# Moving the start addresses of the weight tiles and of x's low part in an attention and feed-forward kernel

## The chip, the cores and the metric

The kernel runs on one core of a Trainium2 chip. The time is device time of one execution in microseconds (us). The unchanged kernel took 599.97 us in the median of three runs (599.84 to 600.01).

The engines are named as the profile names them: PE is the matrix engine (a MATMUL streams columns, a LDWEIGHTS, shown as PEld, loads the stationary operand beforehand), DVE the vector engine, ACT the scalar engine, POOL the general engine, SP the engine that issues the transfers (DMA). Tiles lie in the core's own memory (SBUF, 128 partitions); sums of matmuls lie in PSUM. An address here is the byte within a partition at which a tile begins.

## The reference

Four batches of 768 tokens, eight heads of 64, go through chunked attention: each chunk of 32 queries sees 8 memory keys, 16 keys to its left, its own 32 and 8 to its right, 64 in all. The result, 3072 tokens of 512, is x of a feed-forward layer with 2048 hidden units:

```python
scores = scale * np.matmul(q_c, k_full.transpose(0, 1, 3, 2))
scores = scores - np.max(scores, axis=-1, keepdims=True)
a = np.exp(scores)
a = a / (np.sum(a, axis=-1, keepdims=True) + 1e-09)
out[:, :, c_start:c_end] = np.matmul(a, v_full)
...
h = x @ w_in
g = np.where(pos, h, np.where(neg, 0.0, (h + beta) ** 2 / (4.0 * beta)))
return (g @ w_out).astype(np.float32)
```

## The kernel before

The tokens are cut into six blocks of 512. A block's attention is done in two halves of 256 tokens: scores on PE, softmax on DVE and ACT, a transpose, values on PE, and then x of this half is written to SBUF as two tiles, a rounded high part `xth` (ACT, `x_high`) and the rest `xtl` (DVE, `x_low`). Each half is written by two instructions of DVE, `a` = 0 and 1, whose columns interleave in runs of 32; for the first block (`first_attention`) each of four pieces is written by one instruction, for two of the four groups of heads (`cc`) and one half. In a tile of x the four groups of 512 tokens follow each other.

The feed-forward layer runs over sixteen slices `fc` of 128 hidden units. A step `pe_hidden` is 12 matmuls of 512 columns: weights stand (high with x high, low with x high, high with x low, four groups `cc` each), x streams. After a gate on ACT and DVE, `pe_out` is 12 matmuls in which pieces of the gate's result `gh`, `gl` stand and 512 columns of weights stream. Every weight is held as a high and a low part too: sixteen tiles `w_0` to `w_15` arrive as raw words by DMA and are decoded in place by ACT and DVE (`decode`) into `wr` tiles under the same tags, 8192 bytes in a partition each: 4096 of high, 4096 of low, two of the 32 slices of weights in each (tile 0 holds the first two of `w_in`, the next ones a slice of `w_in` and one of `w_out`).

The order on every engine is written out: a string of names (`FIRST`) up to the end of the second block, a loop over steps after that. In the string, `g` is the first block's attention, `n` the others', `w` the decoding of a tile, `A` and `B` are steps of 256 tokens of the first block (its first and its second half), `J` steps of the whole of it, `C`, `D` and `E` the same of the second block. Nothing reorders it. What an instruction waits for is derived by the tile framework: an instruction that reads or writes a part of a tile waits for the earlier ones that touched parts which overlap it, by the views' offsets and strides as the framework sees them.

SBUF is filled pool after pool, tile after tile: `const` (the identity, then the weight tiles), `xpool` (two buffers each of `xth` and `xtl`), `apool` (attention's tiles), `gpool` (the gate's). The tile `offset` of 128 bytes at the head of `gpool` is never used. Line 63 of the profile is the helper that records all instructions, so groups are told apart by their tiles.

Of the kernel before, what the change touches and what calls it, by code (L numbers as in the profile page):

```python
# [9 lines left out]
F32R = mybir.dt.float32r  # L10
BF16 = mybir.dt.bfloat16
U32 = mybir.dt.uint32
# [4 lines left out]
P = 128  # L17
CHUNK, LEFT, RIGHT = 32, 16, 8
TB = 512
NCH = TB // CHUNK  # L20
NT = TB // P
NEG = -3.0e38
LAG = 2


STARTS = (3, 9)
# [42 lines left out]
def attn_ffn_kernel(ctx: ExitStack, tc: tile.TileContext, first_qk, first_v, qk, vw, w, out):  # L69
# [3 lines left out]
    NP = first_qk.shape[0]  # L73
# [9 lines left out]
    n2 = 2 * DM  # L83

    const = ctx.enter_context(tc.tile_pool(name="const", bufs=1))
    xpool = ctx.enter_context(tc.tile_pool(name="xpool", bufs=2))
# [44 lines left out]
    ws, raw = {}, {}  # L131

    def load_w(i, parts=(0, 1)):
        if i not in raw:
            raw[i] = const.tile([P, 2 * n2], U32, name=f"w_{i}", tag=f"w_{i}")
        a, b = parts[0] * n2, (parts[-1] + 1) * n2
        sp.dma_start(raw[i][:, a:b], w[i, :, a // 2 : b // 2].bitcast(U32))

# [5 lines left out]
    def words(i):  # L144
        pairs = raw[i].rearrange("p (n two) -> p n two", two=2)
        return pairs[:, :, 0], pairs[:, :, 1]

    def decode(i):

        low, u = words(i)  # L150
        high = u.bitcast(F32)

        act.activation(high, high, AF.Copy, scale=2.0**-112)
        yield
        f = apool.tile([P, n2], U32, name="f", bufs=2)
        dve.tensor_scalar(f, u, 3, None, op0=ALU.logical_shift_left)
        yield
        dve.scalar_tensor_tensor(f, low, 29, f, op0=ALU.logical_shift_right, op1=ALU.bitwise_or)
        yield
        dve.scalar_tensor_tensor(f, u, 0x80000000, f, op0=ALU.bitwise_and, op1=ALU.bitwise_or)  # L160
        yield
        f = f.bitcast(F32)
        ws[i] = const.tile([P, 2 * n2], F32R, name=f"wr_{i}", tag=f"w_{i}")
        hi, lo = ws[i][:, 0:n2], ws[i][:, n2 : 2 * n2]
        act.copy(hi, f)
        yield
        dve.tensor_tensor(lo, f, hi.bitcast(F32), op=ALU.subtract)
        yield


    scores_of, prob, prob_t, banks, xts, both = {}, {}, {}, {}, {}, {}

    def x_of(blk):
        if blk not in xts:
            xts[blk] = [xpool.tile([P, NP, TB], F32R, name=n) for n in ("xth", "xtl")]
        return xts[blk]

    def mask(c, s, swapped=False):
# [33 lines left out]
    def first_attention(g):  # L212
# [47 lines left out]
        for r in range(2):  # L260
# [14 lines left out]
        hi, lo = (  # L275
            x[:, 2 * u : 2 * u + 2, half * HT : (half + 1) * HT].rearrange("p r (t q) -> p r t q", t=2)
            for x in x_of(0)
        )
        act.copy(hi, src)
# [68 lines left out]
    def x_views(key, a):  # L348
        blk, half = key
        src = banks[key][:, a].rearrange("p (r t q) -> p r t q", r=NP, t=2)  # L350
        views = []
        for x in x_of(blk):
            x = x[:, :, half * HT : (half + 1) * HT].rearrange("p r (t a q) -> p r t a q", t=2, a=2)
            views.append(x[:, :, :, a])
        return (src, *views)
# [28 lines left out]
    def run(*chains):  # L384

        chains = [c for c in chains if c is not None]
        while chains:
            chains = [c for c in chains if next(c, chains) is not chains]
# [26 lines left out]
    def gating(s):  # L415

        h = hidden.pop(s)
        g = gpool.tile([P, TB], F32, name="gw", tag="gw")
        t = gpool.tile([P, TB], F32, name="gt")
        act.activation(g, h, AF.Relu, bias=0.5, scale=0.5)  # L420
        act.activation(t, h, AF.Relu, bias=-1.0)
        act.activation(g, g, AF.Square)
        gate[s] = (g, t)
# [12 lines left out]
    def gate_low(s):  # L436
        gh, gl = gs[s]
        dve.tensor_tensor(gl, gate.pop(s), gh.bitcast(F32), op=ALU.subtract)
        yield

    def pe_out(s):
        blk, fc = divmod(s, NFC)
        gh, gl = gs.pop(s)
        if fc == 0:
            pairs = [two_banks(f"a{i}", "ps_o") for i in range(NT // 2)]
            acc[blk] = [pairs[t // 2][:, t % 2] for t in range(NT)]
        wh, wl = weights(1, fc, 0), weights(1, fc, 1)
        pe_products(acc[blk], gh, gl, wh, wl, fc)
# [58 lines left out]
    def store(blk):  # L507
        for t in range(NT):
            src = acc[blk][t]
            if t % 2 == 0:  # L510
                ob = apool.tile([P, 2, DM], F32, name="ob", tag="f", bufs=2)
            dst = ob[:, t % 2]
            if t == NT - 1:
                dve.tensor_copy(dst[:, 0 : DM // 2], src[:, 0 : DM // 2])
                act.copy(dst[:, DM // 2 : DM], src[:, DM // 2 : DM])
            elif t % 2:
                act.copy(dst, src)
            else:
                dve.tensor_copy(dst, src)
            r0 = blk * TB + t * P  # L520
            sp.dma_start(out[r0 : r0 + P, :], dst)

    def keep_warm(n):
# [5 lines left out]

    early = [  # L530
        (load_first_qk, 0), (load_first_qk, 1), (load_first_v, 0), (load_w, 0), (load_first_v, 1),
        (load_first_qk, 2), (load_w, 1), (load_first_qk, 3), (load_first_v, 2), (load_first_v, 3),
        (load_w, 2), (load_w, 3), (load_w, 4), (load_qk, 1, 0), (load_v, 1, 0),
    ]
    early += [(load_w, i) for i in range(5, NPW)]
# [9 lines left out]
        "g": first_attention,  # L545
        "n": lambda i: attention((1 + i // 2, i % 2)),
        "w": decode,
    }
    parts = {"A": (0, (0, 1)), "B": (0, (2, 3)), "J": (0, range(NT))}
    parts |= {"C": (1, (0, 1)), "D": (1, (2, 3)), "E": (1, range(NT))}  # L550
    chains = {}
    for name in FIRST.split():
# [4 lines left out]
        if name not in chains:  # L557
            kind, i = name[0], int(name[1:])
# [15 lines left out]
    for s in range(first * NFC, steps):  # L574
# [25 lines left out]
        gating(s)  # L600
        if s - LAG >= first * NFC:
            pe_out(s - LAG)
            if (s - LAG) % NFC == NFC - 1:
                store((s - LAG) // NFC)
        else:
            n, i = LAST // LAG, s - first * NFC
            for name in items[len(items) - LAST :][i * n : (i + 1) * n]:
# [4 lines left out]
    run(gate_low(steps - 1))  # L612
    for s in range(steps - LAG, steps):
        pe_out(s)
# [90 lines left out]
```

## Time and profile before

| what | value |
|---|---|
| median of three runs | 599.97 us |
| the profiled execution | 600.11 us |
| its span, first to last instruction | 598.3 us |
| PE busy | 582.7 us, 97% |
| DVE busy | 325.6 us, 54% |
| ACT busy | 280.3 us, 47% |
| moved by DMA | 55.31 MB |

The page gives each engine's busy time; a view by stretches gives the same for any part of the span; the chain of waits follows the work that ended last back to the start, in pieces; the timeline lists instructions in order of time, equal neighbours merged ("x8"), with the start of the first. The time from one start to the next, over the count between them, is what a matmul costs in a stream: the duration of one is longer, because matmuls overlap.

### The profile page before, as it was taken

To read this page: it belongs to the slowest core of one execution; us is meant where nothing else is said; L and a number is where in the kernel's file an instruction comes from. 1 tells how busy PE (TensorE), PEld (TensorE's weight loads), DVE (VectorE), ACT (ScalarE), POOL (GpSimd) and SP (SyncE) were. 2 spreads that over 40 slices of the span, in tenths; PEclk is the share of its full clock that TensorE was granted. 3 is DMA by queue.
4 is the path that set the end of the run, shared out by engine and by line. 5 is a ranking of instruction groups with operands and counts; after the bars stand their busy time and mean duration, and the time that the engine had idled before them with its cause. 6 is when DMAs were issued, how large, how long until landed. Compare 5 with 4: busy or idle time off the path is not lost.

```text
span 598.3 us, 12265 instructions
## 1 busy us (share of the span) xinstructions
PE 582.7 (97%) x5496; PEld 483.5 (81%) x5496; DVE 325.6 (54%) x466; ACT 280.3 (47%) x503; POOL 0.7 (0%) x6
## 2 busy tenths in 40 slices
PE   5899999999999999999999999999999999999996
PEld 2888888788888888888888888888888888888885
DVE  5999999986474224636423644623564632322222
ACT  2689864554435335444435443434443444543442
POOL 0000000000000000000000000000000000000000
PEclk9999999999999999999999999999999999999999
DMA  8999300424051004012101223200310000100001
GB/s 355 422 418 419 148 1 0 178 82 168 1 177 71 0 1 158 26 65 108 71 1 71 107 71 107 71 1 34 144 71 2 1 2 0 71 0 1 0 1 70
DMA packets 9844, 55.31 MB, mean 92 GB/s; under 512 B 1088, under 2 KB 1088, under 8 KB 5184
## 3 DMA queue, kind: packets, MB, share of 16 engines
q1 hardware_dynamic: 9792, 54.53, 23.6%
q8 instruction: 43, 0.70, 0.5%
q14 instruction: 9, 0.07, 0.0%
HBM read 48.23 MB, written 6.29 MB: 91 GB/s over the span
## 4 chain that ended last, share of the span: by engine, by line
PE 82%; DVE 15%; issue 2%; DMA 1%; ACT 0%; DVEq 0%; ACTq 0%
PE ps_o L63 38%; PE ps_h L63 38%; DVE f L63 6%; PE ps_x L63 3%; DVE wr L63 2%; PE ps_s L63 2%; DVE gw L63 1%; DVE gl L63 1%; DVE pr L63 1%; DVE den L63 1%; DMA qk<-in_first_qk_dram 1%; DVE pt L63 1%; DVE mx L63 1%; DVE xtl L63 0%; DVE rin L63 0%
## 5 line engine op out<-in xcount | busy, mean ns | idle before, releaser
L63 PE MATMUL ps_h<-xth,wr 128*128 128x512 f32 (+1 forms) x832 | 195.6, 377 | 1.1 <-DVE wr L63 1.1
L63 PE MATMUL ps_o<-wr,gh 128*128 128x512 f32 x768 | 194.7, 390 | 0.0
L63 PEld LDWEIGHTS ps_h<-xth,wr 128*128 128x128 f32 x832 | 149.0, 190 | 30.3 <-DVE wr L63 1.5
L63 PEld LDWEIGHTS ps_o<-wr,gh 128*128 128x128 f32 x768 | 143.3, 188 | 29.4
L63 DVE SCALAR_TENSOR_TENSOR gw<-gw,gt 128x512 f32<-128x512 f32 (+1 forms) x104 | 67.2, 649 | 164.9 <-ACT gw L63 164.6
L63 ACT ACTIVATE gw<-ps_h 128x512 f32<-128x512 f32 (+1 forms) x104 | 58.6, 563 | 159.0 <-PE ps_h L63 158.9
L63 PE MATMUL ps_o<-wr,gl 128*128 128x512 f32 x384 | 106.9, 389 | 0.0
L63 PE MATMUL ps_h<-xtl,wr 128*128 128x512 f32 (+1 forms) x416 | 104.8, 374 | 0.0
L63 DVE TENSOR_TENSOR gl<-gw,gh 128x512 fp32r<-128x512 f32 (+1 forms) x104 | 67.4, 649 | 65.8 <-ACT gh L63 65.7
L63 ACT CAST gh<-gw 128x512 fp32r<-128x512 f32 (+1 forms) x104 | 61.1, 590 | 69.9 <-DVE gw L63 69.9
L63 PEld LDWEIGHTS ps_h<-xtl,wr 128*128 128x128 f32 x416 | 75.3, 190 | 13.9
L63 PEld LDWEIGHTS ps_o<-wr,gl 128*128 128x128 f32 x384 | 72.1, 188 | 15.1
L63 ACT ACTIVATE gw<-gw 128x512 f32<-128x512 f32 (+1 forms) x104 | 62.4, 600 | 0.0
L63 ACT ACTIVATE gt<-ps_h 128x512 f32<-128x512 f32 (+1 forms) x104 | 58.3, 561 | 0.0
L63 DVE STREAM_TRANSPOSE pt<-pr 32x512 f32<-32x512 f32 (+1 forms) x60 | 41.2, 698 | 1.3
L63 DVE SCALAR_TENSOR_TENSOR f<-w,f 128x1024 uint32<-128x1024 uint32 x32 | 39.0, 1220 | 0.4
L63 ACT ACTIVATE pr<-pr 128x1024 f32<-128x1024 f32 (+1 forms) x14 | 13.1, 937 | 35.1 <-DVE pr L63 35.0
L63 PEld LDWEIGHTS ps_x<-pt,v 64*64 64x64 f32 x1536 | 25.1, 142 | 5.0 <-issue 3.3
L63 PE MATMUL ps_x<-pt,v 64*64 64x32 f32 x1536 | 26.6, 226 | 1.2 <-ACT pt L63 1.2
L63 ACT CAST xth<-ps_x 128x512 fp32r<-128x512 f32 x24 | 13.1, 591 | 20.6 <-PE ps_x L63 20.6
L63 ACT CAST wr<-f 128x1024 fp32r<-128x1024 f32 x16 | 16.8, 1051 | 11.7 <-DVE f L63 11.7
L63 PEld LDWEIGHTS ps_s<-qk 64*32 64x32 f32 x1536 | 17.1, 112 | 6.1 <-issue 3.1
(27 smaller groups left out, 182.6 us busy)
## 6 DMA issues: line engine op xcount, KB each, us to landing
w<-in_w_dram SPq DMA_DIRECT2D x16, 1024.0 KB, 19.8
qk<-in_qk_dram SPq DMA_DIRECT2D x10, 1536.0 KB, 6.5
v<-in_vw_dram SPq DMA_DIRECT2D x10, 1024.0 KB, 5.5
out_dram<-ob SPq DMA_DIRECT2D x24, 256.0 KB, 2.0
qk<-in_first_qk_dram SPq DMA_DIRECT2D x4, 768.0 KB, 8.7
v<-in_first_v_dram SPq DMA_DIRECT2D x4, 512.0 KB, 12.7
```

Source lines behind the costliest of these rows:

```text
L63: return self.tc.keep_in_program_order(getattr(self.engine, name)(*args, **kwargs))
```

## The change

Every weight tile is made 16 bytes longer than is used, and so is the low part of x, whose used part begins 16 bytes into its tile. The allocator rounds a tile's size up to 32 bytes, so each weight tile begins 8224 bytes behind the one before it in place of 8192.

```diff
+STEP = 4
...
-            raw[i] = const.tile([P, 2 * n2], U32, name=f"w_{i}", tag=f"w_{i}")
+            raw[i] = const.tile([P, 2 * n2 + STEP], U32, name=f"w_{i}", tag=f"w_{i}")[:, 0 : 2 * n2]
...
-        ws[i] = const.tile([P, 2 * n2], F32R, name=f"wr_{i}", tag=f"w_{i}")
+        ws[i] = const.tile([P, 2 * n2 + STEP], F32R, name=f"wr_{i}", tag=f"w_{i}")[:, 0 : 2 * n2]
...
-            xts[blk] = [xpool.tile([P, NP, TB], F32R, name=n) for n in ("xth", "xtl")]
+            low = xpool.tile([P, NP * TB + STEP], F32R, name="xtl")[:, STEP:]
+            xts[blk] = [xpool.tile([P, NP, TB], F32R, name="xth"), low.rearrange("p (c t) -> p c t", c=NP)]
```

In the built programs the starts within 256 bytes are these:

| tiles | before | after |
|---|---|---|
| the sixteen weight tiles | 128, all | 128, 160, 192, 224, 0, 32, ... each 32 further, twice round |
| `xth`, two buffers | 128 | 192 |
| `xtl`, two buffers (used part) | 128 | 144 and 176 |
| `gh`, `gl` and the gate's others | 128 | 192 |

No instruction is added to the arithmetic or taken from it, and on every engine the instructions stand in the order they had. What changes beside the addresses is what some of them wait for. The first place is on DVE, in the second block's second half: the two instructions of `x_low`, and the gate's work around them.

```order
L63 TENSOR_TENSOR gl<-gw,gh 128x256 [waits DVE_49,Activation_49]
L63 SCALAR_TENSOR_TENSOR gw<-gw,gt 128x256 [waits Activation_49]
L63 TENSOR_TENSOR xtl<-ps_x,xth 128x4x2x64 [waits PE_49,Activation_49]
L63 TENSOR_TENSOR xtl<-ps_x,xth 128x4x2x64
L63 TENSOR_TENSOR gl<-gw,gh 128x256 [waits Activation_49]
```

and of the change:

```order
L64 TENSOR_TENSOR gl<-gw,gh 128x256 [waits DVE_49,Activation_49]
L64 SCALAR_TENSOR_TENSOR gw<-gw,gt 128x256 [waits Activation_49]
L64 TENSOR_TENSOR xtl<-ps_x,xth 128x4x2x64 [waits PE_49,Activation_49]
L64 TENSOR_TENSOR xtl<-ps_x,xth 128x4x2x64 [waits DVE_49]
L64 TENSOR_TENSOR gl<-gw,gh 128x256 [waits Activation_49]
```

The second write of x's low part now waits for a count of DVE's own, that of the first write; the same holds for all ten pairs of `x_low`.

The second place is on PE, at the same time in the program. `wr_398`, `wr_542`, `wr_593` and `wr_281` are the decoded tiles 1, 2, 3 and 0. The step with `xth,wr_542` is one of the second block's first half (`C`), the one with `xth,wr_281` behind it the first of its second half (`D`).

```order
L63 MATMUL ps_o<-wr_398,gl 128x512 [waits DVE_49]
L63 MATMUL ps_o<-wr_398,gl 128x512
L63 MATMUL ps_h<-xth,wr_542 128x256 x8
L63 MATMUL ps_h<-xtl,wr_542 128x256 x4
L63 MATMUL ps_o<-wr_542,gh 128x512 x4
L63 MATMUL ps_o<-wr_542,gl 128x512 x2
L63 MATMUL ps_h<-xth,wr_281 128x256 [waits Activation_49]
L63 MATMUL ps_h<-xth,wr_281 128x256 x7
L63 MATMUL ps_h<-xtl,wr_281 128x256 [waits DVE_49]
L63 MATMUL ps_h<-xtl,wr_281 128x256 x3
```

and of the change:

```order
L64 MATMUL ps_o<-wr_398,gl 128x512 [waits DVE_49]
L64 MATMUL ps_o<-wr_398,gl 128x512
L64 MATMUL ps_h<-xth,wr_542 128x256 x8
L64 MATMUL ps_h<-xtl,wr_542 128x256
L64 MATMUL ps_h<-xtl,wr_542 128x256 [waits DVE_49]
L64 MATMUL ps_h<-xtl,wr_542 128x256 x2
L64 MATMUL ps_o<-wr_542,gh 128x512 x4
L64 MATMUL ps_o<-wr_542,gl 128x512 x2
L64 MATMUL ps_h<-xth,wr_281 128x256 [waits Activation_49]
L64 MATMUL ps_h<-xth,wr_281 128x256 x7
L64 MATMUL ps_h<-xtl,wr_281 128x256 x4
```

The wait for the count that the second write of the first place reaches stood at the first step of half two, which reads what was written. It now stands seventeen matmuls earlier, at the second of the four x-low matmuls of a step of half one, whose columns that write doesn't touch; the three x-low matmuls from there on, six of `pe_out` and eight with x high stand behind it.

The third place is on DVE in the first block: the write of x's low part for its second half, groups 0 and 1.

```order
L63 TENSOR_TENSOR pr_275<-pr_275,rin 128x512 [waits DVE_49]
L63 SCALAR_TENSOR_TENSOR f<-w_335,f 128x1024
L63 TENSOR_TENSOR xtl<-ps_x,xth 128x2x256 [waits Activation_49]
L63 SCALAR_TENSOR_TENSOR gw<-gw,gt 128x256
L63 SCALAR_TENSOR_TENSOR f<-w_335,f 128x1024 [waits DVE_49]
```

and of the change:

```order
L64 TENSOR_TENSOR pr_275<-pr_275,rin 128x512 [waits DVE_49]
L64 SCALAR_TENSOR_TENSOR f<-w_335,f 128x1024
L64 TENSOR_TENSOR xtl<-ps_x,xth 128x2x256 [waits PE_49,Activation_49]
L64 SCALAR_TENSOR_TENSOR gw<-gw,gt 128x256
L64 SCALAR_TENSOR_TENSOR f<-w_335,f 128x1024 [waits DVE_49]
```

The write now also waits for a matmul on PE: the second x-low matmul of the hidden step that stands just ahead of it in the program, on the first half's columns.

## The prediction

> **What bounds the kernel now.** I read the busy times first, then the chain of waits where the bound changes hands, the busy times by stretches, and the timeline of the engine found.
>
> ```profile
> span 598.3 us, 12265 instructions
> PE 582.7 (97%) x5496; PEld 483.5 (81%) x5496; DVE 325.6 (54%) x466; ACT 280.3 (47%) x503; POOL 0.7 (0%) x6
> ```
>
> PE is busy nearly throughout, though not always as the bound:
>
> ```profile
> 105.87 1.23 DVE wr L63
> 107.10 0.04 issue
> 107.14 2.11 PE ps_h L63 x8
> ...
> 27.00:107.00 80.00, 77.85 (x739) 65.90 (x738) 79.27 (x103) 59.57 (x104) 0.00 (x0) 1.00 0.49 203
> 107.00:133.00 26.00, 25.86 (x373) 22.29 (x374) 23.95 (x35) 12.80 (x27) 0.00 (x0) 1.00 0.35 132
> 133.00:150.00 17.00, 17.00 (x224) 15.16 (x223) 11.91 (x21) 8.12 (x23) 0.00 (x0) 1.00 0.45 162
> 190.00:598.00 408.00, 403.71 (x3215) 333.40 (x3213) 166.94 (x241) 169.85 (x304) 0.00 (x0) 1.00 0.13 46
> ```
>
> The columns of the stretches are length, then busy time of PE, PEld, DVE, ACT and POOL, the granted clock, the DMA engines' share and GB/s. Up to 107.1 us the chain runs over DVE (79.27 of 80 us busy); from 107.14 it is PE, which works all 17.00 us of 133 to 150 and 25.86 of 26 before. So a delay of DVE counts before 107.1, a delay of PE counts after it, in full, because no pause follows that could take it up.
>
> What does a matmul cost in that stream?
>
> ```profile
> 398.09 1.98 PE L63 MATMUL ps_o<-wr,gh 128*128 128x512 f32 x8
> 399.90 1.07 PE L63 MATMUL ps_o<-wr,gl 128*128 128x512 f32 x4
> 400.81 1.98 PE L63 MATMUL ps_h<-xth,wr 128*128 128x512 f32 x8
> 402.62 1.07 PE L63 MATMUL ps_h<-xtl,wr 128*128 128x512 f32 x4
> 403.53 1.98 PE L63 MATMUL ps_o<-wr,gh 128*128 128x512 f32 x8
> ...
> 29.41 1.22 PE L63 MATMUL ps_h<-xth,wr 128*128 128x256 f32 x8
> 30.46 0.64 PE L63 MATMUL ps_h<-xtl,wr 128*128 128x256 f32 x4
> 30.95 0.49 PE L63 MATMUL ps_h<-ident,pr 128*128 128x128 f32 x3
> ```
>
> From 398.09 to 403.53 start 24 matmuls: 226.7 ns each, the same for those in which weights stand and x streams (2.72 us for 12) and those in which the gate's tiles stand and weights stream (2.72). With 256 columns the four from 30.46 to 30.95 take 0.12 us each (their unrounded starts give 120.0). So 256 columns cost 106.7 ns, and 13.3 ns of each matmul don't depend on its length. That rest is all that an address can take away: whatever it does, 213.3 ns stay.
>
> **The change part by part: addresses.** In the kernel before, all operands of these streams begin at the same byte within 256, so this trace holds no matmul with another distance between what stands and what streams. It does show whether PE's reads suffer from others' accesses to SBUF, which come at all distances:
>
> ```profile
> 170.88 1.98 PE L63 MATMUL ps_h<-xth,wr 128*128 128x512 f32 x8
> 172.69 1.07 PE L63 MATMUL ps_h<-xtl,wr 128*128 128x512 f32 x4
> 173.60 1.98 PE L63 MATMUL ps_o<-wr,gh 128*128 128x512 f32 x8
> 175.41 1.07 PE L63 MATMUL ps_o<-wr,gl 128*128 128x512 f32 x4
> 176.32 0.39 PE L63 MATMUL ps_h<-xth,wr 128*128 128x512 f32 x1
> ...
> 171.04:176.48 5.44, 5.44 (x26) 4.50 (x25) 4.74 (x8) 2.96 (x5) 0.00 (x0) 1.00 0.45 183
> 398.25:417.29 19.04, 19.04 (x86) 15.77 (x85) 4.85 (x7) 8.86 (x16) 0.00 (x0) 1.00 0.00 1
> ```
>
> At 171 to 176 us DVE works 4.74 of 5.44 us and DMA moves 183 GB/s, at 398 to 417 DVE 4.85 of 19.04 and DMA 1 GB/s; 24 matmuls take 5.44 us (170.88 to 176.32) there and 5.44 here (398.09 to 403.53). Traffic that must meet PE's reads in the same memory at changing addresses costs nothing to the nanosecond. I therefore take 13.3 ns for a cost of changing the standing weights, not of addresses, and the change of addresses for 0. The bounds: 13.3 ns gained on every moved matmul, or the slowest run of eight lost:
>
> ```profile
> 113.31 2.12 PE L63 MATMUL ps_h<-xth,wr 128*128 128x512 f32 x8
> 115.27 1.08 PE L63 MATMUL ps_h<-xtl,wr 128*128 128x512 f32 x4
> 116.19 1.98 PE L63 MATMUL ps_o<-wr,gh 128*128 128x512 f32 x8
> ```
>
> behind the switch from scores, where eight take 1.96 us (245 ns, 18.3 over the rule, the refilling of PE among it) and the next four 0.92 (230 ns, 3.3 over): neighbours in kind of what another phase between loads and streams can cost. The matmuls at stake start after 107.14:
>
> ```profile
> L63 PE MATMUL ps_o<-wr,gh 128*128 128x512 f32 x672 | 170.1, 390 | 0.0
> L63 PE MATMUL ps_h<-xth,wr 128*128 128x512 f32 x620 | 155.3, 392 | 1.1 <-DVE wr L63 1.1
> L63 PE MATMUL ps_o<-wr,gl 128*128 128x512 f32 x336 | 93.4, 389 | 0.0
> L63 PE MATMUL ps_h<-xtl,wr 128*128 128x512 f32 x312 | 83.5, 389 | 0.0
> ```
>
> That is 1940; the weights' starts run twice round the eight places within 256, so two tiles of sixteen still agree with x high and the gate's tiles: 14/16, about 1700, change their distance. The bounds are -22.6 us (13.3 ns) and +31 us (18.3 ns), with 0 the value taken.
>
> [...]
>
> DVE, ACT and the DMAs meet other addresses too:
>
> ```profile
> L63 DVE SCALAR_TENSOR_TENSOR f<-w,f 128x1024 uint32<-128x1024 uint32 x32 | 39.0, 1220 | 0.4
> L63 DVE TENSOR_TENSOR pr<-pr,rin 128x1024 f32<-128x1024 f32 x10 | 12.3, 1225 | 0.3
> ACT w L63 <- DMA w<-in_w_dram: 1.2, 2, 1.1
> ```
>
> `f` begins at 0 within 256 and `pr` at 128; 1024 columns with two operands cost DVE 1220 and 1225 ns, so I take 0 for the engines (a bound is those 5 ns in 1225, some 0.3 us of the 79.27 that DVE works while it is the bound). The weight DMAs write as many bytes as before, and all that waits for them waits 1.2 us, in two waits. The upper bound is that these double, 1.2 us; the value is 0, because the loads' lengths stay.
>
> **The waits.** The new tile has 2052 words for 4 groups of 512 and begins 4 words in; the framework no longer sees that parts of it don't overlap. Three waits come of it.
>
> First, PE's at the step of the second block's first half:
>
> ```profile
> 133.23 0.64 PE L63 MATMUL ps_h<-xtl,wr 128*128 128x256 f32 x4
> 133.06 1.29 DVE L63 TENSOR_TENSOR xtl<-ps_x,xth 128x512 fp32r<-128x512 f32 x2 [0.54 <-ACT xth L63]
> ...
> 28.87 0.20 DVE L63 RECIPROCAL rin<-den 128x8 f32<-128x8 f32 x1
> 29.11 0.69 DVE L63 TENSOR_TENSOR pr<-pr,rin 128x512 f32<-128x512 f32 x1
> ```
>
> The second x-low matmul started at 133.23 + 0.12 = 133.35. It will wait for the second of the two writes, which here overlap (1.29 us for both). With the new wait between them the second starts when the first is done and its count is seen: 0.04 us, as from 28.87 + 0.20 = 29.07 to 29.11, where the one needs the other's result. So 133.06 + 0.69 + 0.04 + 0.68 = 134.47, and PE goes on 0.04 later (the "issue" between DVE wr and PE ps_h at 107.10): 134.51. That is 1.16 us of stall. After a pause PE refills: the eight from 29.41 to 30.46 take 1.05 where 8 x 0.12 = 0.96, so 0.09 more. **+1.25 us.** Behind it stand x-low matmuls, six of pe_out and the steps after them, all in the stream without a pause: nothing takes it up. Were the writes 1.16 us earlier, it would cost nothing; that is the lower bound. The upper one is 1.25 + 0.12, if ACT's writes of x high ahead come a little later too.
>
> Second, DVE's at the first block's second half:
>
> ```profile
> 29.72 1.22 DVE L63 SCALAR_TENSOR_TENSOR f<-w,f 128x1024 uint32<-128x1024 uint32 x1
> 30.85 0.68 DVE L63 TENSOR_TENSOR xtl<-ps_x,xth 128x512 fp32r<-128x512 f32 x1
> ```
>
> The write began 0.09 us before the f ahead of it had ended (30.94). It will wait for the second x-low matmul of 30.46, which starts at 30.58 and is over some 0.28 later (0.64 less 3 x 0.12), at 30.86, before the f. What goes is the overlap: **+0.1 us**, on DVE while it is the bound. Bounds 0 and 0.15.
>
> Third, the nine other pairs of x_low lose an overlap of some 0.12 us each on DVE after 107.1, when DVE pauses for hundreds of us in all and PE doesn't wait for it: 0. Were the cover gone, 9 x 0.12 = 1.1 us.
>
> Sum: 1.25 + 0.10 = 1.35 us on the profiled execution's 600.11 gives 601.5; it lies 0.14 over the median, so on 599.97 **601.3 us**, 0.22% more.
>
> **The rivals.** *Collisions at equal starts, now avoided.* For it: 13.3 ns are unexplained, and all operands did begin alike. Against it: other traffic at all distances costs PE nothing. Price: 1700 x 13.3 ns = -22.6 us, so 578.7; a mild form, 3.3 ns, gives -5.6 and 595.7.
>
> *Equal starts were the good case.* Loads and streams that ran in step now don't, and the stream settles at the 230 ns of 115.27 to 116.19: 1700 x 3.3 = +5.6 us, 606.9; it decides from 0.7 ns per matmul on, which outweighs the waits. For it: the rhythm does vary behind switches. Against it: it finds back to 226.7 within a dozen matmuls.
>
> *The waits cost next to nothing*, because the two writes of x low come earlier than I read them or PE makes up for it: 600.0 to 601.1, no change.
>
> **How the numbers follow.** About 0.2%, 1.2 us, is what a measurement of this kernel tells from none: slower begins at 601.2. Forecast (addresses nothing, waits 1.35) 0.45; waits less than that 0.17; equal starts were good 0.20; collisions avoided 0.18. The forecast's own range is 601.2 to 601.6. The range reaches to the mild form of both address rivals, 3.3 ns either way: 595.7 to 606.9, which leaves out about 0.08 above and 0.12 below. Faster 0.18, the same 0.17, slower 0.45 + 0.20 = 0.65.
>
> **What would show it.** Twelve matmuls at 2.72 us in all steps, with tiles of every start: addresses cost nothing; 2.56 would be the first rival, 2.76 and more the second, and steps that differ tile by tile would tell the distances apart. A pause of PE of about 1.2 us near 133 us that ends on DVE xtl, and pairs of xtl that no longer overlap, show the waits. I am wrong if the steps change their length, if no such pause is there, or if the bound changes hands later than 107.3.

## The result, and the profile after

The changed kernel takes 610.89 us in the median (610.59 to 611.11) beside 599.95 us for the kernel before on the same chip: a ratio of 1.0182, interval 1.0165 to 1.0200. It is slower by 10.9 us. The profiled execution took 610.81 us.

First the span and the busy times, of the changed kernel:

```profile
span 609.0 us, 12266 instructions
PE 592.5 (97%) x5496; PEld 483.0 (79%) x5496; DVE 326.6 (54%) x466; ACT 281.1 (46%) x503; POOL 0.7 (0%) x6
```

PE does the same 5496 matmuls and is busy 9.8 us longer (582.7 before); DVE and ACT have grown by 1.0 and 0.8 us. The span has grown by 10.7. Nearly all of it is work of PE that became longer, and little of it waiting. The stretches of the changed kernel show where:

```profile
107.00:133.00 26.00, 26.00 (x373) 22.07 (x372) 24.16 (x35) 13.14 (x28) 0.00 (x0) 1.00 0.36 132
133.00:150.00 17.00, 16.05 (x220) 14.18 (x219) 10.52 (x19) 8.14 (x23) 0.00 (x0) 1.00 0.49 174
190.00:609.00 419.00, 414.39 (x3224) 335.37 (x3222) 168.44 (x242) 171.32 (x307) 0.00 (x0) 1.00 0.12 45
```

Between 107 and 133 PE still did 373 instructions, as before. Between 133 and 150 it is idle for 0.95 us, where it had no pause. And the long rest of the program, from 190 us to the end, has grown from 408 to 419 us with nearly the same PE work in it (3224 instructions, 3215 before), at a granted clock of 1.00 as before. The chain of waits in the long rest, of the changed kernel (start, us, what):

```profile
396.33 2.79 PE ps_h L64 x12
399.13 2.80 PE ps_o L64 x12
401.92 2.81 PE ps_h L64 x12
404.73 2.79 PE ps_o L64 x12
407.52 2.78 PE ps_h L64 x12
410.30 2.80 PE ps_o L64 x12
413.11 2.77 PE ps_h L64 x12
415.88 2.74 PE ps_o L64 x12
```

Behind 190 us every step of twelve matmuls that doesn't follow a switch from the attention's small ones took 2.72 us before, whatever its tile (2.95 to 2.97 behind a switch). In this stretch it takes 2.74 to 2.81 now, and it differs from step to step: 0.06 us more in a typical step, 5 ns per matmul. I took the starts of the single matmuls out of both traces, paired them in the order of the program, and averaged the interval from one start to the next over all matmuls of 512 columns behind 107.1 us that are followed by another such one, without the first interval behind a pause or a switch (18 before, 17 after, some 340 ns each; 1898 and 1900 intervals stay): **227.1 ns before, 232.0 ns after**. For the 1940 matmuls of that kind that is 1940 x 4.9 ns = 9.5 us. The delay of each matmul against its counterpart grows evenly, by about 0.5 us per hundred matmuls of 512 columns, apart from one jump.

The jump is the wait that the prediction named. Timeline of PE and of DVE, the row of the waits, and the chain of waits there, all of the changed kernel:

```profile
133.56 0.28 PE L64 MATMUL ps_h<-xtl,wr 128*128 128x256 f32 x1
134.78 0.62 PE L64 MATMUL ps_h<-xtl,wr 128*128 128x256 f32 x3 [0.95 <-DVE xtl L64]
...
133.31 1.42 DVE L64 TENSOR_TENSOR xtl<-ps_x,xth 128x512 fp32r<-128x512 f32 x2 [0.54 <-ACT xth L64]
...
PEld ps_h L64 <- DVE xtl L64: 1.2, 1, 1.2
...
133.31 0.70 DVE xtl L64
...
134.04 0.70 DVE xtl L64
...
134.78 0.62 PE ps_h L64 x3
```

One x-low matmul starts at 133.56, the next at 134.78, 1.22 us later in place of 0.12; the two writes of x low no longer overlap (1.42 us for the pair in place of 1.29). The delay of PE against the kernel before is 0.33 us just ahead of this pause, 1.55 at 135 us and 10.67 at the end. So 1.2 us are the pause with the refilling behind it, and 9.1 us come after it, which are the 1866 matmuls of 512 columns that stand there, at 4.9 ns each. The other 74 stand ahead of the pause; its end is set by DVE, so what they lose costs nothing. The chain runs over DVE, with a stretch of ACT at 131 us, until the second write ends at 134.74 us, where in the kernel before PE carried it from 107.14 on. On DVE 0.14 us of delay are there from the program's first 10 us on (the traces of other kernels lie between 0.4 us earlier and 0.14 later at that place), and 0.11 us come from the earlier pair of writes of x low, at 108.9 us.

### The profile page after: what moved, and what is told of

The parts are those of the page before. It is cut to its first block, busy times and chain, and to the rows that moved or that the text cites. A ratio compares the mean times of both kernels' runs of the same rounds, so it can differ in the third digit from the quotient of the medians.

```text
span 609.0 us, 12266 instructions
## 1 busy us (share of the span) xinstructions
PE 592.5 (97%) x5496; PEld 483.0 (79%) x5496; DVE 326.6 (54%) x466; ACT 281.1 (46%) x503; POOL 0.7 (0%) x6
## 4 chain that ended last, share of the span: by engine, by line
PE 79%; DVE 17%; issue 2%; DMA 1%; ACT 1%; DVEq 0%; ACTq 0%
PE ps_h L64 37%; PE ps_o L64 36%; DVE f L64 6%; PE ps_x L64 3%; DVE wr L64 2%; PE ps_s L64 2%; DVE gw L64 2%; DVE gl L64 2%; DVE pt L64 1%; DVE pr L64 1%; DVE den L64 1%; DVE mx L64 1%; DMA qk<-in_first_qk_dram 1%; DVE xtl L64 1%; DVE ob L64 0%
## 5 line engine op out<-in xcount | busy, mean ns | idle before, releaser
L64 PE MATMUL ps_o<-wr,gh 128*128 128x512 f32 x768 | 198.4, 395 | 0.0
L64 PE MATMUL ps_h<-xth,wr 128*128 128x512 f32 (+1 forms) x832 | 198.1, 380 | 0.0
L64 PE MATMUL ps_o<-wr,gl 128*128 128x512 f32 x384 | 108.9, 394 | 0.0
L64 PE MATMUL ps_h<-xtl,wr 128*128 128x512 f32 (+1 forms) x416 | 106.8, 378 | 0.9 <-DVE xtl L64 0.9
```

Of the source, the lines that this page charges most:

```text
L64: return self.tc.keep_in_program_order(getattr(self.engine, name)(*args, **kwargs))
```

## The experiments

Three theories stood at the start. *Distance*: what a matmul costs depends on how far apart, within 256 bytes, its standing and its streaming operand begin. *Spacing*: it is the weight tiles' distance from one another, 8224 in place of 8192 bytes, or that steps of different starts follow each other. *Waits*: it is the new waits. A distance is given here as the start of the standing operand less that of the streaming one, within 256. It is 0 for all of these matmuls in the kernel before; in the changed kernel it goes through the multiples of 32 in the steps with x high and in `pe_out`, and through those 16 away from them with x low. The weight tiles lie in memory in the order in which the program first asks for them, which is 0, 13, 1, 14, 15 and then 2 to 12, and not by number.

### Longer spacing, equal starts

The change with 256 in place of 16 bytes: the tiles lie further apart, and all begin alike again.

```diff
-STEP = 4
+STEP = 64
```

> The same change with steps of 256 bytes in place of 16: every weight tile begins 8448 bytes behind the last, x's low part 256 bytes further, so all starts agree within 256 as before; the framework sees no overlap with this size, so the added waits are gone too. Theory D (a matmul costs more when the operand that streams and the operand that is loaded begin at different bytes within 256, by some 5 to 6 ns on average): 600.0 us, twelve matmuls at 2.72 us. Rival S (the spacing of the tiles itself, or that they are parts of longer tiles, costs): about 610 us.

Measured: 599.98 us beside 599.99, ratio 1.0000 (0.9991 to 1.0009). Its chain of waits:

```profile
398.00 2.72 PE ps_o L64 x12
400.72 2.72 PE ps_h L64 x12
```

The steps are back at 2.72 us. Longer tiles and another spacing, 8448 bytes or 33 times 256 from tile to tile, cost nothing that shows; for the loss, the starts within 256 bytes had to differ. The framework sees no overlap with this length either, and the pause near 133 us is gone as well.

### The weights alone

The weights as in the change, x low as before; no wait is added.

```diff
-            low = xpool.tile([P, NP * TB + STEP], F32R, name="xtl")[:, STEP:]
-            xts[blk] = [xpool.tile([P, NP, TB], F32R, name="xth"), low.rearrange("p (c t) -> p c t", c=NP)]
+            xts[blk] = [xpool.tile([P, NP, TB], F32R, name=n) for n in ("xth", "xtl")]
```

> Weight tiles 32 bytes further on from one to the next, x low as before, no added wait. Theory D: 14 of 16 tiles differ from x and from the gate's tiles, 1940 matmuls at a mean of 231.8 ns in place of 226.7: 600.0 + 9.9, about 609.5 us, and no pause of PE near 133 us. Rival X (the shift of x low is what unsettles the stream): 600 us.

Measured: 610.08 us beside 599.99, ratio 1.0166 (1.0149 to 1.0183). Its chain of waits:

```profile
412.25 2.75 PE ps_h L64 x12
415.00 2.79 PE ps_o L64 x12
417.79 2.73 PE ps_h L64 x12
```

The weights' starts alone bring 10.1 us, and the steps differ tile by tile as in the changed kernel: the mean interval is 232.3 ns, and 1940 x 5.2 ns = 10.2 us. With x low moved as well it is 232.0, a little less: moving x low cost nothing further once the weights were moved, beyond its waits.

### The low part of x alone

Only x low begins further on, at 144 and 176; x high, the weights and the gate's tiles stay at 128 (the unused tile ahead of the gate's was cut by 64 bytes for that). The waits are those of the change.

```diff
-            xts[blk] = [xpool.tile([P, NP, TB], F32R, name=n) for n in ("xth", "xtl")]
+            high = xpool.tile([P, NP, TB], F32R, name="xth")
+            low = xpool.tile([P, NP * TB + 4], F32R, name="xtl")[:, 4 : 4 + NP * TB]
+            xts[blk] = [high, low.rearrange("p (c t) -> p c t", c=NP)]
...
-    gpool.tile([P, 32], F32, name="offset", bufs=1)
+    gpool.tile([P, 16], F32, name="offset", bufs=1)
```

> x low alone begins 16 and 48 bytes further within 256 (two buffers), weights, x high and the gate's tiles all at 128 as before; the added waits are there. Theory D: the 312 matmuls of 512 columns that stream x low cost about 6 ns more, 1.9 us, and the waits 1.25: 603.1 us. Rival W (x low's address costs nothing, only its waits): 601.2 us. Rival X (x low unsettles the whole stream): 608 us or more.

Measured: 605.45 us beside 599.99, ratio 1.0090 (1.0075 to 1.0105), more than expected. Timeline of PE:

```profile
406.27 1.10 PE L63 MATMUL ps_h<-xtl,wr 128*128 128x512 f32 x4
407.21 2.00 PE L63 MATMUL ps_o<-wr,gh 128*128 128x512 f32 x8
409.05 1.07 PE L63 MATMUL ps_o<-wr,gl 128*128 128x512 f32 x4
409.95 1.98 PE L63 MATMUL ps_h<-xth,wr 128*128 128x512 f32 x8
411.77 1.09 PE L63 MATMUL ps_h<-xtl,wr 128*128 128x512 f32 x4
412.69 2.00 PE L63 MATMUL ps_o<-wr,gh 128*128 128x512 f32 x8
```

The four x-low matmuls, at a distance of 240 or 208 (x low has two buffers), take 0.94 us (406.27 to 407.21) or 0.92 (411.77 to 412.69) in place of 0.91. But the eight behind them, whose own distance is 0, take 1.84 us (407.21 to 409.05) in place of 1.81 as well; only the four `gl` after that are back at 0.90. One by one the eight take 230, 224, 231, 236, 228, 232, 231 and 227 ns: PE needs about eight matmuls to fall back into its old rhythm. About 0.026 us in each of 78 pairs of steps makes 2.0 us, and 312 x 5.7 ns = 1.8 us for the x-low matmuls themselves (232.4 ns in the mean); with 1.5 us of waits (next experiment) that is 5.3, measured 5.5. The direction was that of the distances; what a disturbed matmul does to its followers was missing from the expectation.

### The waits alone

x low is lengthened so that the framework sees the overlap, and padding puts every start back to 128.

```diff
-            xts[blk] = [xpool.tile([P, NP, TB], F32R, name=n) for n in ("xth", "xtl")]
+            high = xpool.tile([P, NP, TB], F32R, name="xth")
+            low = xpool.tile([P, NP * TB + 4], F32R, name="xtl", tag=f"xtl{blk % 2}", bufs=1)[:, 0 : NP * TB]
+            if blk < 2:
+                xpool.tile([P, 56], F32, name=f"pad{blk}", bufs=1)
+            xts[blk] = [high, low.rearrange("p (c t) -> p c t", c=NP)]
```

> The added waits without any other address: x low in tiles four words longer, filled up so that every start within 256 is as before. The prediction's term: one pause of PE of 1.2 us near 133 us, 601.2 us in all, twelve matmuls at 2.72 us. Rival: PE makes up for the pause later, 600.0 us; or the waits disturb the stream beyond the pause, over 602 us.

Measured: 601.51 us beside 599.99, ratio 1.0025 (1.0016 to 1.0034): 1.5 us. Timeline of PE, then its chain of waits:

```profile
132.99 0.28 PE L63 MATMUL ps_h<-xtl,wr 128*128 128x256 f32 x1
134.39 0.62 PE L63 MATMUL ps_h<-xtl,wr 128*128 128x256 f32 x3 [1.12 <-DVE xtl L63]
```

```profile
396.67 2.72 PE ps_h L63 x12
399.39 2.72 PE ps_o L63 x12
```

The pause is there, 1.40 us from start to start in this kernel (0.12 without the wait), and the steps stay at 2.72. So the waits are one part and the addresses another, and the waits are by far the smaller one.

### One distance for all: 128, and 192

If the distance counts, and not the change of distance from step to step, then a constant distance must cost as much. With 128 bytes ahead of x in its pool, x and the gate's tiles begin at 0 and the weights at 128: all these matmuls have a distance of 128.

```diff
+    xpool.tile([P, 32], F32, name="shift", bufs=1)
```

> One distance for all, other than 0: x and the gate's tiles begin 128 bytes further within 256 than every weight tile; no tile is longer, no wait added, nothing changes from one step to the next. Theory D (each distance has its own steady rhythm, and only 0 gives 226.7 ns): the settled intervals of the staggered kernels at distance 128, alternately 229 and 238 ns, mean 233.3, on all 1940 matmuls: 600.0 + 12.9 = about 613 us, twelve matmuls at 2.80 us. Rival U (the stagger unsettles the stream because the distance changes every twelve matmuls; one that stays is as cheap as 0): 600.0 us, 2.72 us.

And with 64 bytes ahead of x and a longer unused tile ahead of the gate's, x begins at 192, the gate's tiles at 64 and the weights at 128: a distance of 192 for all.

```diff
+    xpool.tile([P, 16], F32, name="shift", bufs=1)
...
-    gpool.tile([P, 32], F32, name="offset", bufs=1)
+    gpool.tile([P, 64], F32, name="offset", bufs=1)
```

> Weights begin 192 bytes further within 256 than x, the gate's tiles 192 further than the weights: one distance of 192 from what streams to what is loaded, everywhere. Theory D: the settled intervals at this distance in the staggered kernels, 226, 229 and 232 ns, mean 229.0: 600.0 + 4.5 = about 604.5 us. Rival U: 600.0 us. If distances had nothing to do with it but only how many bytes apart (64 is as far as 192 going round): as at distance 64, 233.3 ns, 612.9 us.

Measured: at 128, 610.20 us beside 599.93, ratio 1.0170 (1.0155 to 1.0186); at 192, 605.43 us beside 599.93, ratio 1.0095 (1.0080 to 1.0110). The chains of waits, of the kernel at 128 and of the one at 192:

```profile
401.11 2.78 PE ps_h L63 x12
403.89 2.78 PE ps_o L63 x12
```

```profile
398.29 2.77 PE ps_h L63 x12
401.06 2.75 PE ps_o L63 x12
```

In both kernels all weight tiles are 8192 bytes apart, no wait is added and every step has the same starts; still each step takes longer, by an amount that belongs to its distance. That rules out spacing, and the change from step to step, as what is needed. The size at 128 was expected too high, at about 613 us: the mean interval is 232.2 ns, not 233 and more, and 1940 x 5.1 ns = 9.9 us, measured 10.3. At 192 it is 229.9 ns: 5.4 us, measured 5.5.

### All starts moved together

64 bytes ahead of everything: all tiles begin at 192, and all distances stay 0.

```diff
+    const.tile([P, 16], F32, name="shift")
```

> Weights, x and the gate's tiles all begin 64 bytes further within 256, at 192: every distance is 0 as before, only the common start is another. Theory D (distance alone): 600.0 us, twelve matmuls at 2.72 us. Rival (the start itself counts, 128 being a good one): 604 us or more.

Measured: 600.14 us beside 600.10, ratio 1.0004 (0.9995 to 1.0013). Its chain of waits:

```profile
398.23 2.72 PE ps_o L63 x12
400.95 2.72 PE ps_h L63 x12
```

A common shift of 64 bytes costs nothing that shows: of the starts, it is the distance between them that counts in the shifts tried.

### Distances of a few bytes

The decoded weights begin 0, 4, 8 ... 60 bytes further on in their tiles, x and the gate's tiles stay. The distance is 0 to 56 in `pe_hidden`, where weights stand, and 252 to 196 in `pe_out`, where they stream (tile 0 holds weights of `pe_hidden` alone, tile 15 of `pe_out` alone). Here tiles are meant by number.

```diff
-        ws[i] = const.tile([P, 2 * n2], F32R, name=f"wr_{i}", tag=f"w_{i}")
+        ws[i] = const.tile([P, 2 * n2 + 64], F32R, name=f"wr_{i}", tag=f"w_{i}")[:, i : i + 2 * n2]
```

> The decoded weight tiles begin 0, 4, 8 ... 60 bytes further within 256, from tile 0 to tile 15; x and the gate's tiles stay; no wait added. It shows the distances below 64 in steps of 4 for steps of hidden, above 192 for pe_out. If lines of 16 bytes matter: tiles 0 to 3 at 2.72 us for twelve, the others at 2.75 to 2.80, about 608 us in all. If every byte matters: tile 0 alone at 2.72, about 610 us. If the start within 32 or 64 bytes is what counts and these are small: 600 to 603 us. A piece of twelve below 2.72 us would show a distance that is cheaper than 0.

Measured: 609.22 us beside 599.93, ratio 1.0154 (1.0137 to 1.0171); the mean interval of 231.9 ns times 1940 gives 9.3 us, as measured. Its chain of waits:

```profile
221.17 2.72 PE ps_o L63 x12
223.89 2.75 PE ps_h L63 x12
226.64 2.72 PE ps_o L63 x12
229.36 2.79 PE ps_h L63 x12
232.15 2.84 PE ps_o L63 x12
```

A distance of four bytes, 232.7 ns in the table below, is enough to lose the rhythm. From these kernels (the change, the weights alone, the three with a uniform or a fine distance) I read the interval of a matmul of 512 columns at each distance, as the mean over its runs of one kind once the rhythm has settled, in ns:

| distance, bytes | interval |
|---|---|
| 0 | 226.7 |
| 32, 64, 96 | 233.3, 233.3, 234.7 |
| 128 | 232.8 |
| 160, 192, 224 | 233.5, 228.9, 233.4 |
| 4, 8, 12, 16 | 232.7, 230.4, 230.0, 233.3 |
| 20, 24, 28, 36 | 233.3, 230.0, 233.3, 231.7 |
| 40, 44, 48 to 56 | 233.3, 230.0, 233.3 |
| 196, 200, 204, 208 | 226.7, 230.3, 233.3, 233.3 |
| 212, 216, 220, 228 | 230.0, 233.1, 234.8, 226.7 |
| 232, 236, 240, 244 | 233.3, 235.8, 230.2, 228.9 |
| 248, 252 | 233.8, 236.9 |

All lie between 226.7 and 237. Two further distances, 196 and 228, do as well as 0, and none does better. The means often stand for a period: at 128 the intervals alternate between 229 and 238, or repeat after eight or more. The multiples of 32 occur in both kinds of step and at 32, 64, 96, 160 and 224 agree between them within 1 ns. The other distances come from `pe_hidden` up to 56 and from `pe_out` from 196 on, but for the runs of four with x low.

Nor does the distance alone fix the interval. At 36 (`pe_hidden` with tile 9) the stream ran at 233 ns in three of the last four blocks and at 226.8 in the last, and the 231.7 of the table is a mean of the two. The chain of waits of this kernel, that step in the third block and in the last:

```profile
279.42 2.80 PE ps_h L63 x12
563.96 2.72 PE ps_h L63 x12
```

So one distance can have more than one rhythm. What decides which of them the stream takes, no run here tells.

### A second good distance

Is 228 as good as 0 for a whole kind of step? The gate's tiles begin 228 bytes further on, so all of `pe_out` has a distance of 228 and `pe_hidden` keeps 0.

```diff
-        gh = gpool.tile([P, TB], F32R, name="gh", bufs=3)
-        gl = gpool.tile([P, TB], F32R, name="gl", bufs=3)
+        gh = gpool.tile([P, TB + 64], F32R, name="gh", bufs=3)[:, 57 : 57 + TB]
+        gl = gpool.tile([P, TB + 64], F32R, name="gl", bufs=3)[:, 57 : 57 + TB]
```

> The gate's high and low parts begin 28 bytes below the weights within 256 (distance 228), all else as before. In the kernel with steps of 4 bytes this distance settled at 226.7 ns like 0, its neighbours 224 and 232 at 233. Theory D with a rhythm of its own for each distance: pe_out settles at 2.72 us for twelve, with some ns lost while the rhythm changes between hidden (0) and pe_out (228): 600.0 to 602 us. If only 0 is good: 1008 matmuls at 5 to 6 ns more, 605 to 606 us.

Measured: 600.23 us beside 600.10, ratio 1.0003 (0.9993 to 1.0012). Its chain of waits:

```profile
398.33 2.72 PE ps_o L63 x12
401.06 2.72 PE ps_h L63 x12
```

Both kinds of step take 2.72 us. So it isn't equality of the starts alone that is good: `pe_out` keeps the rhythm at 228 too.

### Which two accesses

PE loads the next standing tile while the present matmul streams: in the kernel before, the loads of eight tiles begin at 403.31, 0.22 us ahead of the first matmul that uses them, and the x-low matmuls ahead of it run until 403.69 (timeline):

```profile
402.62 1.07 PE L63 MATMUL ps_h<-xtl,wr 128*128 128x512 f32 x4
403.31 1.77 PEld L63 LDWEIGHTS ps_o<-wr,gh 128*128 128x128 f32 x8
403.53 1.98 PE L63 MATMUL ps_o<-wr,gh 128*128 128x512 f32 x8
```

So "the distance" could be that between a matmul's streaming operand and its own standing tile, or that between it and the tile which is loaded for the next matmul. In runs of one kind both are the same. To part them, the low weights of `w_out` and `gl` were moved 128 bytes further on, first in the order as it is. In `pe_out` the combinations are then high weights with `gh` at 0, low weights with `gh` and high weights with `gl` both at 128.

```diff
-        c0 = part * n2 + j * DM
+        c0 = part * n2 + j * (DM + 32 * part)
...
-        ws[i] = const.tile([P, 2 * n2], F32R, name=f"wr_{i}", tag=f"w_{i}")
-        hi, lo = ws[i][:, 0:n2], ws[i][:, n2 : 2 * n2]
+        ws[i] = const.tile([P, 2 * n2 + 64], F32R, name=f"wr_{i}", tag=f"w_{i}")
+        hi = ws[i][:, 0:n2]
+        lo = ws[i][:, n2 : n2 + 2 * (DM + 32)].rearrange("p (j c) -> p j c", j=2)[:, :, 0:DM]
...
-        gl = gpool.tile([P, TB], F32R, name="gl", bufs=3)
+        gl = gpool.tile([P, TB + 64], F32R, name="gl", bufs=3)[:, 32 : 32 + TB]
```

> The low part of the gate's tiles begins 128 bytes further within 256, and so does the low half of the weights that pe_out streams; all else as before, order as before (four of high with high, four of gate high with weight low, four of gate low with weight high). A matmul's own two operands then differ by 128 in eight of its twelve; what is loaded while it streams (the next one's standing operand) differs from what it streams in 512 of the matmuls of pe_out. Theory N (the load of the next weights meets the stream): 512 x 5.5 ns, the mean loss at 128 in the kernel with one distance of 128, = 2.8 us and some 2 us until the rhythm is found again behind each group, 604 to 605 us. Theory O (a matmul's own two operands count): 743 x 5.5 = 4.1 and the same 2, about 606 us.

Then with the same starts and the two moved combinations by turns: the tile that is loaded next is now, with few exceptions, at a distance of 0 from what streams, while eight of the twelve matmuls of nearly every `pe_out` keep their own distance of 128.

```diff
-        todo = [(t, kind) for kind in kinds for t in range(len(outs))]
+        todo = [(t, kinds[0]) for t in range(len(outs))]
+        todo += [(t, kind) for t in range(len(outs)) for kind in kinds[1:]]
```

> The same addresses as the kernel with the three kinds in a row; only the order within a step of pe_out differs: four of high with high, then gate high with weight low and gate low with weight high by turns. A matmul's own operands differ by 128 in as many as there (743), but what is loaded next always begins at the byte within 256 at which the running stream begins (24 exceptions). Theory N: as before the change, 600.0 us. Theory O: about as the kernel with the kinds in a row, 604 to 606 us.

And this order alone, with the starts of the kernel before, as a control:

> Control: the order by turns in pe_out with all addresses as before. Both theories: 600.0 us; if the order itself costs or gains something, it shows here and is taken off the kernel with the turns.

Measured beside 600.01 us: in the old order 605.96, ratio 1.0102 (1.0087 to 1.0117); by turns 604.39, ratio 1.0073 (1.0056 to 1.0090); the control 599.96, ratio 1.0001 (0.9991 to 1.0010). The chains of waits, of the old order and of the turns:

```profile
401.19 2.76 PE ps_o L63 x12
403.95 2.76 PE ps_h L63 x12
```

```profile
400.55 2.75 PE ps_o L63 x12
403.30 2.74 PE ps_h L63 x12
```

The mean intervals are 230.1 ns (1940 x 3.0 = 5.9 us, measured 6.0) and 229.3 (4.3, measured 4.4). Neither reading holds alone. If only the next load counted, the turns would cost next to nothing; they cost 4.4 us. If only a matmul's own tile counted, its settled interval would be the 233 ns that the old order shows; by turns it is 230.0 (in a pattern of 226, 234 and 230). Both overlaps may take part. In the turns the streaming operands' own starts also alternate by 128 from one matmul to the next, and no run has that alone. Which accesses count is left open. Here too the neighbours suffer: `pe_hidden`, whose starts are those of the kernel before in fifteen of sixteen slices, takes 2.74 to 2.76 us.

## Why the prediction was wrong

The forecast was 601.3 us, with 595.5 to 607.0; the time is 610.89, slower as forecast, outside the range.

**What bounds the kernel** was right behind the pause and not ahead of it. Behind it each ns of a matmul counts in full: in the eight kernels whose time moved by addresses, 1940 x the mean interval's growth, with the waits where there are any, gives the measured difference within 0.4 us. Ahead of it the added wait makes DVE the bound of the changed kernel up to 134.74 us, and "the bound changes hands later than 107.3" was one of the prediction's own signs of being wrong. It costs little here, because only 74 of the 1940 matmuls stand in that stretch.

**The waits** were right in size. PE's pause: predicted 1.25 us, 1.16 of stall and 0.09 of refilling. By the delay of the matmuls it measured 1.11 and 0.12 in the changed kernel, and 1.28 and 0.10 in the kernel with the waits alone, which took 1.5 us more in all where the sum was 1.35. Two smaller readings fail. The nine other pairs were put at 0, as standing where PE doesn't wait for DVE; the first of them, at 108.9 us, stands on DVE's chain to the pause and adds 0.11 us to DVE's delay in both kernels. And the 0.1 us on DVE in the first block doesn't follow from the times beside it: the awaited matmul was to be over at 30.86, and the `f` whose end is overlapped ended at 30.94. Timeline of DVE, changed kernel, then the same write in the kernel with x low alone:

```profile
29.85 1.22 DVE L64 SCALAR_TENSOR_TENSOR f<-w,f 128x1024 uint32<-128x1024 uint32 x1
30.99 0.68 DVE L64 TENSOR_TENSOR xtl<-ps_x,xth 128x512 fp32r<-128x512 f32 x1
...
31.03 0.69 DVE L63 TENSOR_TENSOR xtl<-ps_x,xth 128x512 fp32r<-128x512 f32 x1 [0.29 <-PE ps_h L63]
```

In the changed kernel the write still begins 0.08 us before the `f` ahead of it has ended, as it did before (0.09), and the wait costs nothing. In the other kernel the matmul came later, and DVE stands for 0.29 us. So what this wait costs depends on how far PE has come by then. The eight pairs behind the pause cost nothing that shows.

**The addresses** are the step that failed: "I therefore take 13.3 ns for a cost of changing the standing weights, not of addresses, and the change of addresses for 0." It rested on one observation: traffic of DVE and of the DMAs, at all distances, leaves 24 matmuls at 5.44 us (DVE busy 4.74 of 5.44 us, DMA 183 GB/s). The observation is right, but it speaks of other engines against PE. What the change moves is PE's two operands against each other, and of that the trace of before held no instance, as the prediction itself said. Being undisturbed by others was taken for being undisturbed by itself. The moved starts cost 4.9 ns on each of 1940 matmuls, and the table of distances has 226.7 to 236.9 ns for the same matmul. Whether the reads of the two operands meet at the memory or the intervals come from a timing inside PE, no run here tells.

**The rivals.** The right one was the second, "Equal starts were the good case". It had been given 0.20 and was mis-sized: 3.3 ns on 1700 matmuls, 5.6 us, where 4.9 ns on 1940 was measured. The 3.3 came from a row behind a switch (230 ns), and that is one of the intervals that occur, but many distances give 233 and more. And 14 of 16 tiles was too low a share, since x low has a distance of its own in all tiles and matmuls at a good distance take about eight to find their rhythm after a bad one (224 to 236 ns in the kernel with x low alone). What spoke against the rival, that the stream "finds back to 226.7 within a dozen matmuls", was read at distance 0 and says nothing of others. The upper bound of 18.3 ns held (10.2 was the largest of the settled means), so the price was within the bounds that the prediction itself named, +31 us; the range was cut at the mild form of either sign. The first rival, collisions at equal starts, is refuted as far as tried: no distance in the table gives less than 226.7. Whether the 13.3 ns that remain at distance 0 have to do with addresses at all stays open.

**What would show it** did its work: "2.76 and more the second" rival; "steps that differ tile by tile would tell the distances apart". In the stretch shown the steps read 2.74 to 2.81.

## What to carry to other kernels

Where PE is the bound and each matmul has a new standing tile, look at where the two operands begin within 256 bytes: put both at the same byte, the one distance that kept the rhythm in both kinds of step here (226.7 ns, up to 236.9 at others), and compare the length of a step in the chain before and after any change that moves tiles, also one that only adds padding or a small tile ahead of a pool (128 bytes ahead of x cost 10.3 us, 64 bytes ahead of everything nothing). And a trace in which a resource is undisturbed by other engines says nothing of how an engine's own accesses meet; where the trace has no instance of a thing, the range has to reach the bounds.

## What the runs showed of the hardware that I had not expected

The interval of a matmul of 512 columns of 32-bit words, each with a new standing tile of 128 columns, depends on the distance of its operands' starts within 256 bytes, in steps as fine as the 4 bytes tried: 226.7 ns at 0, 196 and 228 (the latter two seen with the gate's tiles standing only), up to 236.9 at 252. The dependence isn't smooth: 228 gives 226.7, 232 gives 233.3 and 252 gives 236.9. A common shift of all tiles by 64 bytes changes nothing. At one distance the stream can have more than one rhythm: 233 ns or 226.8 at 36. A run at another distance leaves its trace on the matmuls behind it: with x low alone moved, about eight take 224 to 236 ns until they are back at 226.7, 0.026 us more in all.
